# Decode attention with a gate and a Mish layer: all eight kv heads loaded alike, the dense layer's weights behind them, and wo split over three loads

## The chip, the cores and the metric

The kernel runs on one core of one Trainium2 chip. The metric is the device time of one execution in microseconds (us), the median of three runs. TensorE (PE in the profile) does the matmuls and the transposes, VectorE (DVE), ScalarE (ACT) and GpSimd (POOL) the rest, and SyncE (SP) issues every DMA. All inputs lie in HBM and are read once.

## The reference

Two tokens (B = 2, one position each) pass through an attention over the last W = 4096 positions of a cache and, beside it, through a dense layer with the Mish function; a sigmoid gate mixes the two.

```python
g = _sigmoid((x * gate_w).sum(-1, keepdims=True))
# attention: 32 query heads, 8 kv heads, head size 128, model size 512
q = (x @ wq).reshape(B, Sq, Hq, Dh)...
scores = jnp.einsum("bhqd,bhkd->bhqk", q, k) * (Dh ** -0.5)
o = jnp.einsum("bhqk,bhkd->bhqd", _softmax(scores), v)
a = o.reshape(B, Sq, Hq * Dh) @ wo
# dense layer: 512 -> 1792 -> 512
h = jnp.einsum("bsd,df->bsf", x, w1) + b1
b = jnp.einsum("bsf,fd->bsd", h * jnp.tanh(softplus(h)), w2)
return g * a + (1 - g) * b
```

Everything is 32-bit floating point, so the inputs that have to be moved are 91.24 MB.

## The kernel before

**Loads.** Everything large goes through one pool of three tiles of 64 KB on each of the 128 partitions (`stream`, the helper `load`). A `load` makes a tile and issues one DMA on SP for each of its parts. The eleven tiles come in this order: wq (two parts), kv0 to kv6 (one part of 64 KB rows each, keys in the first half, values in the second), then `w12`, which holds w1 and ten of the fourteen pieces of w2 (one part of 48 KB rows), then `kv7` in two parts of 32 KB rows (keys, values), then `wo` in three parts of 32, 24 and 8 KB rows (16, 12 and 4 query heads). The last four pieces of w2 are three more DMAs (4, 2 and 2 KB rows) into the room left behind in `w12`'s tile. With three tiles, the DMA of a tile waits until PE has read the tile three places ahead of it: w12's waits for kv4, kv7's for kv5, wo's for kv6. The table `CUTS` says how w2 is cut, `WO` how wo is cut (in groups of four query heads).

**A kv head.** `scores` makes the four score products `sc` (16 matmuls, in four column groups of PE that run side by side), the maximum `mx` on DVE and the exponentials `p` on ACT; `turned` transposes `p` on PE into `pp` and copies it to `pT` on ACT; `values` makes `o` (16 matmuls), and after each second head folds two heads into `od` on DVE. Each 32-bit matmul is two PE instructions in the profile, so 16 matmuls are x32 there.

**The dense layer.** `hidden` multiplies w1 into `hp` (16 matmuls), copies it on ACT (`hs`), transposes it (`ht`), and then runs a chain of small operations, mostly on POOL (`e`, `ho`, `nu`, `de`), that ends in the padded activations `actT` and `act2` (both in the tile `padded`).

**Joining the heads.** The chunks of each row of scores have their own maxima. `tops` transposes `mx` on PE into `mt`, finds the common maximum (`mj`, `top` on DVE), subtracts it on POOL (`ms`) and takes exponentials on ACT; `factors` transposes `ms` into `ft` and makes `kf` and `kl` on DVE; `shares` sums on PE into `lp` and makes `r` on DVE and POOL; `outputs` multiplies `od` by `kf` on PE into `ol` and writes the scaled heads `oT` (in `padded`) on DVE.

**The end.** `project` adds 32 query heads times wo and ten pieces of activation times w2 (`middle`) into `acc`, in four column groups, one for each index modulo 4. ACT copies `acc` to `asum`; `finish` adds the last four pieces of w2 and `asum` into `fin`, DVE copies it to `res`, and SP stores it once the last loads have landed.

**Order.** The engines run their instructions in program order; `pin` keeps the marked matmuls as written, the rest is placed by the framework's scheduler. In this kernel the work on w1 (`hidden`) comes ahead of kv7, and the ten `middle` pieces, `tops`, `factors` and `shares` are written by hand between the steps of kv7.

Of the kernel before, what the change touches and what calls it, by code (L numbers as in the profile page):

```python
# [8 lines left out]
F32 = mybir.dt.float32  # L9
AF = mybir.ActivationFunctionType  # L10
ALU = mybir.AluOpType
AX = mybir.AxisListType

P = 128
B = 2
D = 512
HQ = 32
HKV = 8
REP = HQ // HKV
# [6 lines left out]
NT = 4  # L26
Q = 32
RS = Q // B
BH = B * REP
F = 1792  # L30
DC = D // P
# [3 lines left out]
CHUNK = 8192  # L35
# [1 line left out]
SMALL = DC * B + DC + FC  # L37
SCALE = DH ** -0.5
CAP = 20.0
CUTS = (0, 10, 12, 13, 14)  # L40
WO = (0, 4, 7, 8)
ROWS = (24, 104)
WIDE = 2 * Q - B


@with_exitstack
def decode_kernel(ctx: ExitStack, tc: tile.TileContext, res, stored, small, wqh, wqt, kv_in, w12, k7, v7, wo, w2, out):
    nc = tc.nc

    stream = ctx.enter_context(tc.tile_pool(name="stream", bufs=3))  # L50
# [8 lines left out]
    def load(name, *parts):  # L59
        t = stream.tile([P, 2 * CHUNK], F32, tag="s", name=name)  # L60
        x = 0
        for cols, src in parts:
            loads.append(nc.sync.dma_start(t[:, x : x + cols], src))  # L63
            x += cols
        return t
# [12 lines left out]
    for j in range(2, NJ):  # L78
# [6 lines left out]
                            axis=AX.X, op=ALU.add)  # L85
# [54 lines left out]

    pin = tc.keep_in_program_order

    def scores(kv, t):
        sc = ps_s.tile([P, 512], F32, tag="sc", name=f"sc{kv}")
        for m in range(BN):
            for j in range(NJ):
                nc.tensor.matmul(sc[Q * j : Q * j + Q, :], qz[:, kv, m * Q : m * Q + Q],  # L147
                                 t[:, (m * NJ + j) * 512 : (m * NJ + j + 1) * 512],
                                 start=(m == 0), stop=(m == BN - 1))
        nc.vector.tensor_reduce(mx[:, kv : kv + 1], sc, axis=AX.X, op=ALU.max, negate=True)  # L150
        p = work.tile([P, 512], F32, tag="p", name=f"p{kv}")
        nc.scalar.activation(p, sc, AF.Exp, bias=mx[:, kv : kv + 1], accum_out=ls[:, kv : kv + 1])  # L152
        return p

    def turned(kv, p):
        pp = ps_1.tile([P, NT, P], F32, tag="pt", name=f"pp{kv}")
        pT = single.tile([P, NT, P], F32, tag="pT", name=f"pT{kv}")
        for c in range(NT):
            pin(nc.tensor.transpose(pp[:, c, :], p[:, c * P : (c + 1) * P], ident))  # L159
        nc.scalar.copy(pT, pp)  # L160
        return pT

    def softmax(kv, t):
        return turned(kv, scores(kv, t))

    pair = [None]

    def values(kv, pT, t, c0=0, c1=NT):
        if kv % 2 == 0:
            pair[0] = ps_1.tile([P, 2, BN * DH], F32, tag="o", name=f"o{kv}")  # L170
        o = pair[0][:, kv % 2, :]
        for c in range(c0, c1):
            for j in range(NJ):
                pin(nc.tensor.matmul(o[Q * j : Q * j + Q], pT[:, c, Q * j : Q * j + Q],  # L174
                                     t[:, (c * NJ + j) * 512 : (c * NJ + j + 1) * 512],
                                     start=(c == 0), stop=(c == NT - 1)))
        if kv % 2 and c1 == NT:
            wide = [P, 2 * BN, DH]
            om = single.tile(wide, F32, tag="om", name=f"om{kv}")
            ov = om.rearrange("p (k m) d -> p k m d", m=BN)  # L180
            nc.vector.tensor_tensor(  # L181
                ov, pair[0].rearrange("p k (m d) -> p k m d", m=BN),
                pick[:, None, :, None].to_broadcast([P, 2, BN, DH]), op=ALU.mult)
            nc.vector.tensor_reduce(od[:, kv - 1 : kv + 1], ov.rearrange("p k m d -> p k d m"),  # L184
                                    axis=AX.X, op=ALU.add)
# [34 lines left out]
        nc.gpsimd.tensor_tensor(r, r, g[:, None, :, None].to_broadcast([P, HKV, B, REP]), op=ALU.mult)  # L220
        return r

    def outputs(ol, kf, r, k0, k1):
        for kv in range(k0, k1):
            pin(nc.tensor.matmul(ol[:, kv].rearrange("p b h -> p (b h)"), od[:, kv, :], kf[:, kv, :],  # L225
                                 start=True, stop=True))
        nc.vector.tensor_tensor(
            oT.rearrange("p (k h) (b x) -> p k b h x", h=REP, x=RS)[:, k0:k1, :, :, 0],
            ol[:, k0:k1], r[:, k0:k1], op=ALU.mult)

    def hidden(t):
        w = t[:, : DC * F].rearrange("p (c f) -> p c f", c=DC)
        hp = ps_s.tile([P, FG * P], F32, tag="sc", name="hp")
        for c in range(DC):
            for j in range(NJ):
                n = min(FG, FC - j * FG) * P
                nc.tensor.matmul(hp[Q * j : Q * j + Q, :n], x32[:, c, :],  # L237
                                 w[:, c, j * FG * P : j * FG * P + n],
                                 start=(c == 0), stop=(c == DC - 1))
        hs = work.tile([P, FG * P], F32, tag="p", name="hs")  # L240
        nl = (FC - (NJ - 1) * FG) * P
        nc.scalar.copy(hs[:, :nl], hp[:, :nl])
        nc.scalar.copy(hs[: Q * (NJ - 1), nl:], hp[: Q * (NJ - 1), nl:])
        ht = ps_1.tile([P, FG, NJ, Q], F32, tag="pt", name="ht")

        def m(name):
            return const.tile([P, FC, B], F32, name=name)

        h, e, nu, de, ho = (m(x) for x in ("h", "e", "nu", "de", "ho"))
        for k in range(FG):  # L250
            nj = len(range(k, FC, FG))
            nc.tensor.transpose(ht[:, k, :nj, :].rearrange("p j r -> p (j r)"),
                                hs[: Q * nj, k * P : (k + 1) * P], ident[: Q * nj, : Q * nj])
        for j0, j1, nk in ((0, NJ - 1, FG), (NJ - 1, NJ, FC - (NJ - 1) * FG)):
            f0, f1 = j0 * FG, (j1 - 1) * FG + nk
            nc.vector.tensor_tensor(  # L256
                h[:, f0:f1, :].rearrange("p (j k) b -> p j k b", k=nk),
                ht[:, :nk, j0:j1, ::RS].rearrange("p k j b -> p j k b"),
                b1[:, f0:f1].rearrange("p (j k) -> p j k", k=nk)[:, :, :, None]
                .to_broadcast([P, j1 - j0, nk, B]), op=ALU.add)  # L260
        nc.gpsimd.tensor_scalar_min(e, h, CAP)  # L261
        nc.scalar.activation(e, e, AF.Exp)
        nc.gpsimd.tensor_tensor(ho, h, omg[:, None, :].to_broadcast([P, FC, B]), op=ALU.mult)
        nc.gpsimd.tensor_scalar_add(nu, e, 2.0)
        nc.gpsimd.tensor_tensor(nu, nu, e, op=ALU.mult)
        nc.gpsimd.tensor_scalar_add(de, nu, 2.0)
        nc.vector.reciprocal(de, de)
        nc.gpsimd.tensor_tensor(nu, nu, de, op=ALU.mult)
        nc.gpsimd.tensor_tensor(actT[:, :, ::RS], nu[:, : CUTS[1]], ho[:, : CUTS[1]], op=ALU.mult)
        nc.gpsimd.tensor_tensor(act2[:, :, Q - B : Q], nu[:, CUTS[1] :], ho[:, CUTS[1] :], op=ALU.mult)  # L270

    queries(0, wq_t[:, :CHUNK])
    queries(1, wq_t[:, CHUNK:])

    for kv in range(HKV - 1):
        t = load(f"kv{kv}", (2 * CHUNK, kv_in[kv]))
        pT = softmax(kv, t[:, :CHUNK])
        values(kv, pT, t[:, CHUNK:])
    w12_t = load("w12", (DC * F + CUTS[1] * D, w12))
    last = load("kv7", (CHUNK, k7), (CHUNK, v7))  # L280

    def flat(src, cuts, size):
        for f0, f1 in zip(cuts, cuts[1:]):
            yield (f1 - f0) * size, src[f0 * size * P : f1 * size * P].rearrange("(p x) -> p x", p=P)

    wo_t = load("wo", *flat(wo, WO, REP * D))
    x = DC * F + CUTS[1] * D
    for cols, src in flat(w2, [f - CUTS[1] for f in CUTS[1:]], D):
        loads.append(nc.sync.dma_start(w12_t[:, x : x + cols], src))
        x += cols  # L290
    hidden(w12_t)

    acc = ps_1.tile([P, D], F32, tag="acc", name="acc")
    fin = ps_1.tile([P, P], F32, tag="fin", name="fin")
# [17 lines left out]

    def middle(f0, f1):
        for f in range(f0, f1):
            x = DC * F + f * D
            pin(project(f % NJ, actT[:, f, :], w12_t[:, x : x + D], n_of[f % NJ]))

    p = scores(HKV - 1, last[:, :CHUNK])
    middle(0, CUTS[1] // 2)
    ms = tops()  # L320
    pT = turned(HKV - 1, p)
    middle(CUTS[1] // 2, CUTS[1])
    kf, kl = factors(ms)
    values(HKV - 1, pT, last[:, CHUNK:], 0, 1)
    r = shares(kl)
    values(HKV - 1, pT, last[:, CHUNK:], 1, NT)
    ol = ps_1.tile([P, HKV, B, REP], F32, tag="q", name="ol")
    outputs(ol, kf, r, 0, HKV - 2)
    outputs(ol, kf, r, HKV - 2, HKV)
    for x in range(HQ):  # L330
        project(x % REP, oT[:, x, :], wo_t[:, x * D : (x + 1) * D], n_of[x % REP])
    asum = work.tile([P, D], F32, tag="p", name="asum")
    nc.scalar.copy(asum, acc)

    def output(i):
        for f in range(CUTS[i], CUTS[i + 1]):
            x = DC * F + f * D
            finish(act2[:, f - CUTS[1], :], w12_t[:, x : x + D])

    output(1)  # L340
# [71 lines left out]
```

## Time and profile before

| | us |
|---|---|
| median of 3 runs (219.44 to 219.54) | 219.47 |
| the profiled execution's own time | 219.29 |
| its span, first to last instruction | 217.4 |
| last load lands, last `fin` matmuls wait for it | 215.0 |

The page gives, for each engine, its busy time and its share of the span; the chain that ended last, followed back from the last instruction; and groups of instructions by line with the idle time before them and what ended it. In a timeline row the first number is the start in us from the span's start, the second the duration, and a bracket at the end holds the idle time before it and its releaser. PEclk is the TensorE clock that was granted, 1.00 being full speed.

### The profile page before, as it was taken

What the parts mean: (1) busy time and instruction counts of PE and PEld (TensorE: products, weight loads), DVE (VectorE), ACT (ScalarE), POOL (GpSimd) and SP (SyncE); (2) the same over time, 40 slices, a digit from 0 to 9 for tenths busy, and PEclk for the clock granted to TensorE, in tenths of its full rate; (3) what the DMA queues carried; (4) which work ended last, traced back from release to release, by engine and by line L of the source; (5) the groups of instructions that cost most, each with busy time, mean ns of one, the idle gap of its engine ahead of it and who ended that gap; (6) DMA issues with size and microseconds to landing.
All of it is one profiled execution on the core that took longest, in us unless ns stands there. A gap on an engine that the chain in (4) does not pass through costs nothing.

```text
span 217.4 us, 1803 instructions
## 1 busy us (share of the span) xinstructions
PE 120.3 (55%) x804; PEld 34.5 (16%) x804; DVE 21.5 (10%) x33; ACT 15.6 (7%) x34; POOL 8.0 (4%) x30
## 2 busy tenths in 40 slices
PE   0000798377046609543873754287066972997766
PEld 0000322112011102101120210012011220233212
DVE  0000000010001230100105010010501000025100
ACT  2000001011001000200020020002001010030001
POOL 7000000000000000000000000000000003010000
PEclk9999999879959985995669699669758697699699
DMA  9797988898989899989998999899999899999993
GB/s 362 338 506 338 581 386 386 386 570 386 398 386 567 377 398 398 555 386 398 398 555 377 398 410 543 386 398 410 488 434 434 359 464 404 455 410 443 430 383 136
DMA packets 2838, 91.38 MB, mean 420 GB/s; under 512 B 448, under 2 KB 528, under 8 KB 912
## 3 DMA queue, kind: packets, MB, share of 16 engines
q1 hardware_dynamic: 2832, 91.28, 97.5%
q8 instruction: 6, 0.10, 0.2%
HBM read 91.24 MB, written 0.04 MB: 420 GB/s over the span
## 4 chain that ended last, share of the span: by engine, by line
DMA 76%; PE 18%; ACT 2%; DVE 1%; SPq 1%; issue 1%; ACTq 0%
DMA kv<-in_kv 60%; DMA wo<-in_wo 16%; PE sc L147 9%; PE o L174 6%; PE acc L299 2%; ACT p L152 1%; DVE mx L150 1%; PE pp L159 1%; ACT pT L160 1%; PE fin L309 1%; SPq L63 1%; SPq L69 0%; DVE res L350 0%; ACTq L160 0%; ACTq L152 0%
## 5 line engine op out<-in xcount | busy, mean ns | idle before, releaser
L147 PE MATMUL sc<-kv,qz 128*32 128x512 f32 x256 | 47.3, 907 | 49.0 <-DMA kv<-in_kv 44.2
L174 PE MATMUL o<-kv,pT 128*32 128x512 f32 x256 | 32.4, 647 | 5.1 <-ACT pT L160 5.1
L127 PE MATMUL qp<-wq,x 128*32 128x512 f32 x64 | 11.9, 790 | 23.0 <-POOL x L91 23.0
L147 PEld LDWEIGHTS sc<-kv,qz 128*32 128x32 f32 x256 | 10.5, 157 | 83.7 <-DMA kv<-in_kv 49.8
L150 DVE TENSOR_REDUCE mx<-sc 128x1 f32<-128x512 f32 x8 | 5.5, 692 | 102.3 <-PE sc L147 102.3
L152 ACT ACTIVATE p<-sc,mx 128x512 f32<-128x512 f32 x8 | 5.5, 687 | 126.4 <-DVE mx L150 126.4
L159 PE MATMUL pp<-ident,p 128*128 128x128 f32 x32 | 5.2, 285 | 11.6 <-ACT p L152 11.6
L174 PEld LDWEIGHTS o<-kv,pT 128*32 128x32 f32 x256 | 7.8, 118 | 23.2 <-issue 16.4
L299 PE MATMUL acc<-wo,padded 128*32 128x512 f32 x64 | 8.9, 705 | 2.3 <-DMA wo<-in_wo 2.3
L184 DVE TENSOR_REDUCE od<-om 128x256 f32<-128x1024 f32 x4 | 7.5, 1883 | 0.1
L127 PEld LDWEIGHTS qp<-wq,x 128*32 128x32 f32 x64 | 2.5, 136 | 29.0 <-POOL x L91 23.0
L181 DVE TENSOR_TENSOR om<-o,pick 128x1024 f32<-128x1024 f32 x4 | 4.9, 1224 | 21.6 <-PE o L174 21.6
L159 PEld LDWEIGHTS pp<-ident,p 128*128 128x128 f32 x32 | 3.4, 141 | 18.4 <-ACT p L152 18.4
L261 POOL TENSOR_SCALAR e<-h 128x28 f32<-128x28 f32 x1 | 0.3, 285 | 151.3 <-DVE h L256 151.3
L160 ACT COPY pT<-pp 128x512 f32<-128x512 f32 x8 | 4.7, 586 | 5.8 <-PE pp L159 5.8
L299 PE MATMUL acc<-w,padded 128*32 128x512 f32 x20 | 3.8, 597 | 0.0
L237 PE MATMUL hp<-w,x 128*32 128x512 f32 (+1 forms) x32 | 3.6, 540 | 0.0
L299 PEld LDWEIGHTS acc<-wo,padded 128*32 128x32 f32 x64 | 2.1, 126 | 8.3 <-issue 4.4
L225 PE MATMUL ol<-kf,od 128*128 128x8 f32 x16 | 2.1, 259 | 2.2 <-DVE od L184 2.2
L225 PEld LDWEIGHTS ol<-kf,od 128*128 128x128 f32 x16 | 1.9, 191 | 3.1 <-DVE od L184 2.3
L116 DVE RECIPROCAL g<-g 128x2 f32<-128x2 f32 x1 | 0.2, 166 | 22.5 <-POOL g L115 22.5
L133 PE MATMUL qt<-ident,qs 128*128 128x128 f32 x8 | 1.3, 286 | 1.4 <-ACT qs L130 1.4
(65 smaller groups left out, 29.8 us busy)
## 6 DMA issues: line engine op xcount, KB each, us to landing
wq<-in_wqt SPq DMA_DIRECT2D x1, 7168.0 KB, 21.4
w<-in_w SPq DMA_DIRECT2D x1, 6144.0 KB, 41.0
kv<-in_k SPq DMA_DIRECT2D x1, 4096.0 KB, 30.7
kv<-in_v SPq DMA_DIRECT2D x1, 4096.0 KB, 40.0
wo<-in_wo SPq DMA_DIRECT2D x1, 4096.0 KB, 28.7
wo<-in_wo SPq DMA_DIRECT2D x1, 3072.0 KB, 35.6
wq<-in_wqh SPq DMA_DIRECT2D x1, 1024.0 KB, 4.9
wo<-in_wo SPq DMA_DIRECT2D x1, 1024.0 KB, 37.5
```

Of the source, the lines that this page charges most:

```text
L127: nc.tensor.matmul(qp[Q * k : Q * k + Q, :], x32[:, c, :], w[:, c, k, :], start=(c == 0), stop=(c == DC - 1))
L147: nc.tensor.matmul(sc[Q * j : Q * j + Q, :], qz[:, kv, m * Q : m * Q + Q], t[:, (m * NJ + j) * 512 : (m * NJ + j + 1) * 512], start=(m == ...
L150: nc.vector.tensor_reduce(mx[:, kv : kv + 1], sc, axis=AX.X, op=ALU.max, negate=True)
L152: nc.scalar.activation(p, sc, AF.Exp, bias=mx[:, kv : kv + 1], accum_out=ls[:, kv : kv + 1])
L159: pin(nc.tensor.transpose(pp[:, c, :], p[:, c * P : (c + 1) * P], ident))
L160: nc.scalar.copy(pT, pp)
L174: pin(nc.tensor.matmul(o[Q * j : Q * j + Q], pT[:, c, Q * j : Q * j + Q], t[:, (c * NJ + j) * 512 : (c * NJ + j + 1) * 512], start=(c == 0 ...
L181: nc.vector.tensor_tensor(ov, pair[0].rearrange("p k (m d) -> p k m d", m=BN), pick[:, None, :, None].to_broadcast([P, 2, BN, DH]), op=ALU ...
L184: nc.vector.tensor_reduce(od[:, kv - 1 : kv + 1], ov.rearrange("p k m d -> p k d m"), axis=AX.X, op=ALU.add)
L225: pin(nc.tensor.matmul(ol[:, kv].rearrange("p b h -> p (b h)"), od[:, kv, :], kf[:, kv, :], start=True, stop=True))
L237: nc.tensor.matmul(hp[Q * j : Q * j + Q, :n], x32[:, c, :], w[:, c, j * FG * P : j * FG * P + n], start=(c == 0), stop=(c == DC - 1))
L299: return nc.tensor.matmul(acc[Q * j : Q * j + Q, :], lhsT, rhs, start=(n_col[j] == 1), stop=(n_col[j] == n))
```

## The change

kv7 becomes a tile like the others: one DMA of 64 KB rows right behind kv6. `w12` comes behind it, as one DMA of 54 KB rows: w1, then the first four query heads of wo (one kv head's group, `WO[0]` = 1), then nine pieces of w2. The other 28 query heads of wo are two DMAs of 40 and 16 KB rows (20 and 8 heads), and the last five pieces of w2 three DMAs of 6, 2 and 2 KB rows. `scores` and `turned` become one function again, and the hand-written order around kv7 goes: the program is now kv7, `hidden`, `tops`, `factors`, `shares`, `outputs` (all eight heads at once), then the matmuls into `acc` with `middle` behind the first four heads.

```diff
-CUTS = (0, 10, 12, 13, 14)
-WO = (0, 4, 7, 8)
+CUTS = (0, 9, 12, 13, 14)
+WO = (1, 6, 8)
...
+AHEAD = DC * F + WO[0] * REP * D
...
-    for kv in range(HKV - 1):
+    for kv in range(HKV):
         t = load(f"kv{kv}", (2 * CHUNK, kv_in[kv]))
         pT = softmax(kv, t[:, :CHUNK])
         values(kv, pT, t[:, CHUNK:])
-    w12_t = load("w12", (DC * F + CUTS[1] * D, w12))
-    last = load("kv7", (CHUNK, k7), (CHUNK, v7))
+    w12_t = load("w12", (AHEAD + CUTS[1] * D, w12))
...
-    wo_t = load("wo", *flat(wo, WO, REP * D))
-    x = DC * F + CUTS[1] * D
+    wo_t = load("wo", *flat(wo, [f - WO[0] for f in WO], REP * D))
+    x = AHEAD + CUTS[1] * D
...
     hidden(w12_t)
+    kf, kl = factors(tops())
+    outputs(kf, shares(kl))
...
-    p = scores(HKV - 1, last[:, :CHUNK])
-    middle(0, CUTS[1] // 2)
-    ms = tops()
-    pT = turned(HKV - 1, p)
-    middle(CUTS[1] // 2, CUTS[1])
-    kf, kl = factors(ms)
-    values(HKV - 1, pT, last[:, CHUNK:], 0, 1)
-    r = shares(kl)
-    values(HKV - 1, pT, last[:, CHUNK:], 1, NT)
-    ol = ps_1.tile([P, HKV, B, REP], F32, tag="q", name="ol")
-    outputs(ol, kf, r, 0, HKV - 2)
-    outputs(ol, kf, r, HKV - 2, HKV)
+    first = WO[0] * REP
     for x in range(HQ):
-        project(x % REP, oT[:, x, :], wo_t[:, x * D : (x + 1) * D], n_of[x % REP])
+        w = w12_t[:, DC * F + x * D :] if x < first else wo_t[:, (x - first) * D :]
+        if x == first:
+            middle(0, CUTS[1])
+        pin(project(x % REP, oT[:, x, :], w[:, :D], n_of[x % REP]))
```

PE before, from the end of `hidden` to the products with wo (`kv_499` is kv7's tile, `w_497` is w12's; a row counts matmuls, not the two instructions of each):

```order
L252 MATMUL ht<-ident,hs 128x96 x2
L147 MATMUL sc_553<-kv_499,qz 32x512 x16
L299 MATMUL acc<-w_497,padded 32x512 x5
L189 MATMUL mt<-ident,mx 8x128
L159 MATMUL pp_589<-ident,p_571 128x128 x4
L299 MATMUL acc<-w_497,padded 32x512 x5
L205 MATMUL ft<-ident,ms 128x8
L174 MATMUL o_480<-kv_499,pT_590 32x512 x4
L216 MATMUL lp<-kl,ones 128x64
L174 MATMUL o_480<-kv_499,pT_590 32x512 x12
L225 MATMUL ol<-kf,od 128x8 x8
L299 MATMUL acc<-wo,padded 32x512 x32
```

PE with the change, from the end of `hidden` to the end of the program (`w_545` is w12's tile):

```order
L247 MATMUL ht<-ident,hs 128x96 x2
L184 MATMUL mt<-ident,mx 8x128
L200 MATMUL ft<-ident,ms 128x8
L211 MATMUL lp<-kl,ones 128x64
L221 MATMUL ol<-kf,od 128x8 x8
L295 MATMUL acc<-w_545,padded 32x512 x13
L295 MATMUL acc<-wo,padded 32x512 x28
L305 MATMUL fin<-w_545,padded 32x128 x12
L305 MATMUL fin<-asum,padded 32x128 x4
L305 MATMUL fin<-w_545,padded 32x128 x8
```

All of kv7's matmuls have gone from between these rows to a place ahead of `hidden`, and the products with w2 that stood between them now stand, nine of them, behind `ol`. PE at that earlier place, with the change (`kv_497` is kv7's tile now):

```order
L148 MATMUL sc_499<-kv_497,qz 32x512 x16
L157 MATMUL pp_519<-ident,p_517 128x128 x4
L169 MATMUL o_480<-kv_497,pT_520 32x512 x16
L232 MATMUL hp<-w_545,x_93 32x512 x3
L232 MATMUL hp<-w_545,x_93 32x256
```

The product with w1 stands behind kv7, and before it stood ahead of it. POOL with the change, from the first operation of the Mish chain to the last of `shares`:

```order
L256 TENSOR_SCALAR e<-h 128x28
L258 TENSOR_TENSOR ho<-h,omg 128x28
L259 TENSOR_SCALAR nu<-e 128x28
L193 TENSOR_TENSOR ms<-ms,top 8x16x4
L260 TENSOR_TENSOR nu<-nu,e 128x28
L193 TENSOR_TENSOR ms<-ms,top 8x16x4
L261 TENSOR_SCALAR de<-nu 128x28
L263 TENSOR_TENSOR nu<-nu,de 128x28
L264 TENSOR_TENSOR padded<-nu,ho 128x18
L265 TENSOR_TENSOR padded<-nu,ho 128x5x2
L215 TENSOR_TENSOR r<-r,g 128x64
```

The two subtractions into `ms` now stand among the operations of the Mish chain; before, they came behind all of them. On SP the two rows of kv7 become one row ahead of w12's, and the three rows of wo become two.

More of the change, by code (lines that the diff above doesn't have):

```diff
@@ L39, with decode_kernel @@
 CAP = 20.0
-CUTS = (0, 10, 12, 13, 14)
-WO = (0, 4, 7, 8)
+CUTS = (0, 9, 12, 13, 14)
+WO = (1, 6, 8)
 ROWS = (24, 104)
 WIDE = 2 * Q - B
+AHEAD = DC * F + WO[0] * REP * D
 @with_exitstack
-def decode_kernel(ctx: ExitStack, tc: tile.TileContext, res, stored, small, wqh, wqt, kv_in, w12, k7, v7, wo, w2, out):
+def decode_kernel(ctx: ExitStack, tc: tile.TileContext, res, stored, small, wqh, wqt, kv_in, w12, wo, w2, out):
     nc = tc.nc
@@ L141, in decode_kernel, with softmax @@
     pin = tc.keep_in_program_order
-    def scores(kv, t):
+    def softmax(kv, t):
         sc = ps_s.tile([P, 512], F32, tag="sc", name=f"sc{kv}")
@@ L152, in scores @@
         nc.scalar.activation(p, sc, AF.Exp, bias=mx[:, kv : kv + 1], accum_out=ls[:, kv : kv + 1])
-        return p
-    def turned(kv, p):
         pp = ps_1.tile([P, NT, P], F32, tag="pt", name=f"pp{kv}")
@@ L161, in turned, with values @@
         return pT
-    def softmax(kv, t):
-        return turned(kv, scores(kv, t))
     pair = [None]
-    def values(kv, pT, t, c0=0, c1=NT):
+    def values(kv, pT, t):
         if kv % 2 == 0:
@@ L171, in values @@
         o = pair[0][:, kv % 2, :]
-        for c in range(c0, c1):
+        for c in range(NT):
             for j in range(NJ):
@@ L176, in values @@
                                      start=(c == 0), stop=(c == NT - 1)))
-        if kv % 2 and c1 == NT:
+        if kv % 2:
             wide = [P, 2 * BN, DH]
@@ L221, in shares, with outputs @@
         return r
-    def outputs(ol, kf, r, k0, k1):
-        for kv in range(k0, k1):
+    def outputs(kf, r):
+        ol = ps_1.tile([P, HKV, B, REP], F32, tag="q", name="ol")
+        for kv in range(HKV):
             pin(nc.tensor.matmul(ol[:, kv].rearrange("p b h -> p (b h)"), od[:, kv, :], kf[:, kv, :],
@@ L227, in outputs @@
         nc.vector.tensor_tensor(
-            oT.rearrange("p (k h) (b x) -> p k b h x", h=REP, x=RS)[:, k0:k1, :, :, 0],
-            ol[:, k0:k1], r[:, k0:k1], op=ALU.mult)
+            oT.rearrange("p (k h) (b x) -> p k b h x", h=REP, x=RS)[:, :, :, :, 0], ol, r, op=ALU.mult)
     def hidden(t):
@@ L273, in decode_kernel @@
     queries(1, wq_t[:, CHUNK:])
-    for kv in range(HKV - 1):
+    for kv in range(HKV):
         t = load(f"kv{kv}", (2 * CHUNK, kv_in[kv]))
@@ L314, in middle @@
         for f in range(f0, f1):
-            x = DC * F + f * D
+            x = AHEAD + f * D
             pin(project(f % NJ, actT[:, f, :], w12_t[:, x : x + D], n_of[f % NJ]))
-    p = scores(HKV - 1, last[:, :CHUNK])
-    middle(0, CUTS[1] // 2)
-    ms = tops()
-    pT = turned(HKV - 1, p)
-    middle(CUTS[1] // 2, CUTS[1])
-    kf, kl = factors(ms)
-    values(HKV - 1, pT, last[:, CHUNK:], 0, 1)
-    r = shares(kl)
-    values(HKV - 1, pT, last[:, CHUNK:], 1, NT)
-    ol = ps_1.tile([P, HKV, B, REP], F32, tag="q", name="ol")
-    outputs(ol, kf, r, 0, HKV - 2)
-    outputs(ol, kf, r, HKV - 2, HKV)
+    first = WO[0] * REP
     for x in range(HQ):
-        project(x % REP, oT[:, x, :], wo_t[:, x * D : (x + 1) * D], n_of[x % REP])
+        w = w12_t[:, DC * F + x * D :] if x < first else wo_t[:, (x - first) * D :]
+        if x == first:
+            middle(0, CUTS[1])
+        pin(project(x % REP, oT[:, x, :], w[:, :D], n_of[x % REP]))
     asum = work.tile([P, D], F32, tag="p", name="asum")
@@ L336, in output @@
         for f in range(CUTS[i], CUTS[i + 1]):
-            x = DC * F + f * D
+            x = AHEAD + f * D
             finish(act2[:, f - CUTS[1], :], w12_t[:, x : x + D])
@@ L381 @@
     wo = a("A_wo").reshape(HQ, DH, D)
+    wo_0 = wo[: WO[0] * REP].transpose(1, 0, 2).reshape(P, WO[0] * REP * D)
     wo = np.concatenate([wo[f * REP : t * REP].transpose(1, 0, 2).ravel()
@@ L389 @@
         "wqt": c(wq[:, HEAD:]),
-        "kv": c(np.concatenate([kt[:-1], vt[:-1]], axis=2)),
-        "w12": c(np.concatenate([w1, w2_0], axis=1)),
-        "k7": c(kt[-1]),
-        "v7": c(vt[-1]),
+        "kv": c(np.concatenate([kt, vt], axis=2)),
+        "w12": c(np.concatenate([w1, wo_0, w2_0], axis=1)),
         "wo": c(wo),
```

## Prediction

> **What bounds the kernel now.** I read the page first: its span, the DMA queues and the chain that ended last.
>
> ```profile
> span 217.4 us, 1803 instructions
> q1 hardware_dynamic: 2832, 91.28, 97.5%
> DMA 76%; PE 18%; ACT 2%; DVE 1%; SPq 1%; issue 1%; ACTq 0%
> ```
>
> The loads keep the 16 DMA engines busy for 97.5% of the span. The kernel is one stream of 91.28 MB, and PE works on what has landed. So two questions decide: when each tile lands, and how much work is left behind the last tiles. For the landings, here are rows of SP's timeline, of the list of DMA issues (the last number is the time from issue to landing) and of the chain.
>
> ```profile
> 132.79 0.33 SPq L63 DMA_DIRECT2D w<-in_w  x1
> 152.70 0.33 SPq L63 DMA_DIRECT2D kv<-in_k  x1
> 153.08 0.54 SPq L63 DMA_DIRECT2D kv<-in_v  x1
> 174.13 1.28 SPq L63 DMA_DIRECT2D wo<-in_wo  x3
> ```
> ```profile
> w<-in_w SPq DMA_DIRECT2D x1, 6144.0 KB, 41.0
> kv<-in_k SPq DMA_DIRECT2D x1, 4096.0 KB, 30.7
> kv<-in_v SPq DMA_DIRECT2D x1, 4096.0 KB, 40.0
> wo<-in_wo SPq DMA_DIRECT2D x1, 4096.0 KB, 28.7
> out<-res SPq DMA_DIRECT2D x1, 40.0 KB, 1.5
> ```
> ```profile
> 116.11 43.20 DMA kv<-in_kv
> 174.50 35.56 DMA wo<-in_wo
> 210.11 3.64 PE acc L299 x32
> 213.78 0.65 PE fin L309 x16
> 214.46 1.05 PE fin L309 x24
> 215.53 0.29 DVE res L350
> ```
>
> kv6 lands at 116.11 + 43.20 = 159.3, w12 at 132.79 + 41.0 = 173.8, kv7's keys at 183.4 and values at 193.1, the first part of wo at 174.13 + 28.7 = 202.8, the second at 174.50 + 35.56 = 210.1. Every step is rows times about 0.302 us for each KB of the row: 48 KB in 14.5, 32 KB in 9.6 to 9.7, 24 KB in 7.2. All were issued 28 us or more before they landed, so the stream has no gap.
>
> The end shows how well PE keeps up. `acc` ends at 210.11 + 3.64 = 213.75, and this row shows that the last weights of `fin` still waited for the last load, 215.0:
>
> ```profile
> 215.04 0.16 PEld L309 LDWEIGHTS fin<-w,padded 128*32 128x32 f32 x8 [0.21 <-DMA w<-in_w]
> ```
>
> So before the change PE is just ahead of the stream, with 0.2 us to spare. The end is 215.0 plus the last `fin`, `res` and the store.
>
> **The change, in the stream.** The same bytes move, in two DMAs fewer. What a DMA costs beside its bytes is bounded by the rows above: keys and values together took 193.1 - 173.8 = 19.3 us for 64 KB, a rate at which w12's 48 KB would take 14.5, as they did. Two fewer save between 0 and 0.2 us; I take 0.1. The landings after the change follow from 0.302 us a KB: kv7 at 159.3 + 19.3 = 178.6, **w12 at 178.6 + 16.3 = 194.9**, wo's first part (40 KB) at 207.0, its second (16 KB) at 211.8, the last load at 214.9. SP issues kv7, w12 and wo when it issued w12, kv7 and wo (PE's release of kv4, kv5, kv6 does not move), so the queue stays full.
>
> The Trainium skill, "DMA: Bandwidth & Descriptors", section on the anatomy of one DMA, fits a fixed cost of about 2.0 us for each DMA, on the path that software feeds. By it, one DMA fewer ahead of w12 would move all that follows by 2 us; keys and values, at 9.6 to 9.7 us each beside 19.3 for a whole kv tile, show no such cost in this queue.
>
> **The change, on PE.** w12 used to land at 173.8, ahead of kv7, so `hidden` and ten `middle` pieces were done while kv7 came in. Now it lands at 194.9, last but for wo, and everything below waits for it in a row, with 20.0 us to the last landing. Rows of PE's timeline (start, duration), of DVE's and of POOL's:
>
> ```profile
> 159.36 6.51 PE L147 MATMUL sc<-kv,qz 128*32 128x512 f32 x32 [6.72 <-DMA kv<-in_kv]
> 168.89 5.17 PE L174 MATMUL o<-kv,pT 128*32 128x512 f32 x32 [0.73 <-ACT pT L160]
> 173.88 3.60 PE L237 MATMUL hp<-w,x 128*32 128x512 f32 x32
> 177.99 0.65 PE L252 MATMUL ht<-ident,hs 128*128 128x128 f32 x4 [0.51 <-ACT hs L242]
> 189.71 1.88 PE L299 MATMUL acc<-w,padded 128*32 128x512 f32 x10
> 191.52 0.27 PE L189 MATMUL mt<-ident,mx 128*8 128x128 f32 x1
> 194.00 0.22 PE L205 MATMUL ft<-ident,ms 8*128 8x8 f32 x1
> 195.15 0.43 PE L216 MATMUL lp<-kl,ones 128*128 128x64 f32 x2
> 198.22 1.50 PE L225 MATMUL ol<-kf,od 128*128 128x8 f32 x12
> 201.90 0.61 PE L225 MATMUL ol<-kf,od 128*128 128x8 f32 x4 [2.17 <-DVE od L184]
> ```
> ```profile
> 194.51 0.22 DVE L211 TENSOR_TENSOR kl<-kf,ls 128x64 f32<-128x64 f32 x1
> 199.84 0.24 DVE L227 TENSOR_TENSOR padded<-ol,r 128x48 f32<-128x48 f32 x1 [0.25 <-PE ol L225]
> ```
> ```profile
> 192.76 0.59 POOL L198 TENSOR_TENSOR ms<-ms,top 8x64 f32<-8x64 f32 x2 [10.98 <-DVE top L196]
> ```
>
> kv7 itself is not on the path: kv6 took from 159.3 to 168.89 + 5.17 = 174.1, 14.8 us, so kv7 is through by 178.6 + 14.8 = 193.4 at the latest. From 194.9 on, step by step:
>
> 1. `hp`: 3.6 us at full clock. The same 32 instructions of `sc` took 6.5 where the clock was 0.50, so the other end is 6.8. I take **5.5**, for the reason under the clock below.
> 2. `hs` and `ht`: from `hp`'s end, 177.48, to `ht`'s, 178.64: **1.15**.
> 3. `mt` to `ft`: `ft` began 2.5 us after `mt` began. Now `ms` shares POOL with the Mish chain: its two subtractions (0.59 back to back) stand behind three operations and have a fourth between them, which adds about 0.5; the `mt` itself is ready when `ht` ends. I take 2.7 from `ht`'s end.
> 4. `ft` to `kl`'s end: 0.73; the reciprocal of the Mish chain may stand ahead of `kf` on DVE, 0.1 more. So `lp` begins 3.55 after `ht`.
> 5. `ol`: its first instruction comes 0.3 behind `lp`'s first, twelve took 1.50, sixteen take 1.95. These were hidden behind `om` and wo's landing before; now the product with wo waits for all of them. Then the scaling on DVE, 0.24 and a gap. `oT` stands **6.1** after `ht` (5.7 to 6.6 if the interleaving on POOL costs less or more). The `r` branch, 0.43 of `lp` and two short operations, is done a microsecond earlier.
> 6. `acc`: four matmuls on different column groups run side by side, so 32 instructions are 8 slots of 0.43 (3.60 us), and five pieces take 4 slots (1.88 us), the fifth being alone. 4 heads, 9 pieces and 28 heads are 2 + 6 + 14 = 22 slots: 9.6 us at full clock. By then wo's first part has landed (207.0); its second (211.8) is there before PE needs it. I take **10.8**. Queued behind are all of `fin`, `asum`, `res` and the store.
> 7. From `acc`'s end: `asum` and the `fin` matmuls, 214.46 - 213.75 = 0.71, then 1.05 less the 0.21 of waiting, then from 215.51 to 217.4: **3.4**.
>
> **The clock.** TensorE's clock is granted in steps of 3.41 us in this trace. I laid windows on these steps; the columns are the stretch, its length, PE's busy time and instructions, the granted clock, the DMA share and GB/s.
>
> ```profile
> 182.25:185.66 3.41, 2.17 (x12) 0.50 1.07 461
> 185.66:189.08 3.42, 3.42 (x20) 0.50 1.00 426
> 199.32:202.73 3.41, 1.02 (x8) 1.00 0.99 425
> 202.73:206.14 3.41, 3.31 (x16) 0.50 1.00 432
> 206.14:209.56 3.42, 1.95 (x20) 1.00 0.93 393
> 209.56:212.97 3.41, 2.86 (x28) 1.00 0.99 406
> ```
>
> A stretch with 1.02 us of work at full clock is followed by half, one with 1.95 by full; at half clock 2.17 is not enough to get full back, 3.31 is. With the change PE rests 1.5 us or more ahead of `hp`, and has little to do for the 7.2 us of steps 2 to 5 (`ht`, `mt`, `ft`, `lp`, `ol`: 3.5 us together). So I expect `hp` at half clock for part of its way (5.5) and `acc` to begin with some 2.4 us at half, which costs half of that, 1.2. Where the steps fall against the work is not known, and this is the larger part of the range.
>
> The Trainium skill, "TensorE: Matmul & The Clock Gate", Part 1, has the clock go to half after at least one idle window of about 3.4 us. Here PE rested only from 199.7 to 201.9 (rows of `ol`), 2.2 us, and half was granted at 202.73 all the same, so by this trace a thinly used window is enough. By the page's rule `acc` would start at full clock, since no step from 2 to 5 leaves PE idle for 3.4 us; that is a rival below.
>
> **Sum.** 194.9 + 5.5 + 1.15 + 6.1 + 10.8 + 3.4 = 221.9 for the span, against 217.4. The profiled execution took 219.29, 1.9 more than its span, and the median is 0.2 above it: 221.9 + 2.1 = **224.0**. With all low ends (3.6, 5.7, 9.6) it is 220.5; with all high ends (6.8, 6.6, and 13.0 for `acc` with 6.8 us at half) 228.0.
>
> **The rivals.**
>
> - *PE keeps full clock* through `hp` and `acc` (3.6 and 9.6): 194.9 + 3.6 + 1.15 + 6.1 + 9.6 + 3.4 = 218.8, time 220.9. For it: a short rest may leave a step busy enough, as 206.14 shows; against it: 199.32. This is also where the page's rule leads when PE's rest ahead of `hp` stays short. Chance 0.10.
> - *Half clock for long*, `hp` all at half and `acc` for two steps (6.8 and 13.0): 225.4, time 227.5. For it: a step that is half full stays at half (182.25). Chance 0.10.
> - *The stream still sets the end*, that is, PE's row fits between w12's landing and the last load: 217.3, time 219.4, not slower. Its place is step 6, and it decides from this point: `acc` must end by about 213.8, 18.9 us behind w12, where the low ends of steps 1 to 6 add up to 20.1. It needs steps 3 to 5 to take 4.5 us instead of 6.1, at full clock throughout. Before the change they took 8.3 us from `mt` (191.52) to the first scaling (199.84), with kv7's matmuls in between, so little speaks for it. Chance 0.06, of which 0.02 for a gain over 0.2% from the two DMAs saved and a luckier stream.
> - *Fewer DMAs speed the stream* by the page's 2 us ahead of w12: 222.0. Against it: 9.6 to 9.7 beside 19.3. Chance 0.02.
> - *The forecast*, 222.3 to 225.7 with the clock somewhere between: 0.72.
>
> **How the numbers follow.** The range goes from 220.8, the full clock throughout, to 226.2; it leaves out the longest half clock (0.10) and the stream (0.06). A measurement of this kernel can tell about 0.2% from no change. Faster by more than that 0.02, within it 0.04, slower 0.94.
>
> **What would show it.** In the profile after: `hp` starts at about 194.9 and waits for `w<-in_w`; `acc<-w` starts between 205.5 and 209.5 and waits for DVE's `padded`; `acc<-wo` waits for no load or hardly; the last load lands at about 214.9 with no matmul waiting for it; PEclk is 0.50 in a step near 196 to 200 and in one near 206 to 210. The prediction is wrong if `acc` ends before 214, or if w12 lands well away from 194.9.

## The result and the profile after

The changed kernel takes 225.72 us (median of 6 executions, 224.65 to 227.76), the kernel before 219.45 (219.21 to 219.54): a ratio of 1.0294, 95% interval 1.0247 to 1.0341. It is slower by about 6.3 us. The profiled execution of the changed kernel took 224.65 us, the fastest of the six, with a span of 222.8. In the ratios and medians below, single executions more than 1.5% above the fastest of their kernel are left out (225.46, 225.9, 244.07 and 575.63 us).

The page after, with the same three rows as before:

```profile
span 222.8 us, 1812 instructions
q1 hardware_dynamic: 2544, 91.28, 95.2%
DMA 70%; PE 24%; ACT 2%; DVE 1%; POOL 1%; issue 1%; SPq 0%; ACTq 0%; DVEq 0%
```

The same 91.28 MB keep the DMA engines busy for the same time, but of a longer span, and PE's share of the chain has gone up from 18 to 24%. The end of the chain that ended last, in order of time (start, duration, what):

```profile
151.80 43.18 DMA w<-in_w
195.03 3.69 PE hp L232 x11
...
199.16 0.67 PE ht L247 x4
...
202.25 0.24 PE ft L200
...
203.15 0.42 PE lp L211 x2
203.59 0.57 DVE r L214
204.20 3.38 PE ol L221 x16
207.68 0.28 DVE padded L223
208.00 11.32 PE acc L295 x80
219.34 0.59 ACT asum L321
219.98 0.91 PE fin L305 x24
220.91 0.29 DVE res L338
```

From w12's landing at 151.80 + 43.18 = 194.98 on there is no DMA left in the chain: the steps follow each other without a load between them. Before, the chain went from kv6 through wo's second part, landing at 210.07. The loads, from SP's timeline and the list of DMA issues (the last number is issue to landing):

```profile
171.79 0.81 SPq L64 DMA_DIRECT2D wo<-in_wo  x2
172.65 1.41 SPq L283 DMA_DIRECT2D w<-in_w  x3
```
```profile
wo<-in_wo SPq DMA_DIRECT2D x1, 5120.0 KB, 35.3
w<-in_w SPq DMA_DIRECT2D x2, 256.0 KB, 41.3
```

wo's first part landed at 171.79 + 35.3 = 207.1, and the last pieces of w2 some 41.3 us after issues between 173 and 174, about 215, as before. The stream is as long as it was; `acc` is still at work 4 us later.

The clock in windows of its 3.41 us steps (columns as in the prediction):

```profile
194.23:197.64 3.41, 2.61 (x28) 1.00 1.25 541
197.64:201.05 3.41, 1.78 (x14) 1.00 0.94 408
201.05:204.47 3.42, 0.90 (x6) 1.00 0.89 383
204.47:207.88 3.41, 3.10 (x16) 0.50 0.91 392
207.88:211.30 3.42, 3.30 (x16) 0.50 0.96 408
211.30:214.71 3.41, 3.41 (x36) 1.00 0.67 263
```

`hp` ran at full clock in this execution. The thin step 201.05 to 204.47 (0.90 us of work) was followed by half clock, and so was the next one, although `ol` filled 3.10 us of it.

### The profile page after: what moved, and what is told of

It reads as the page before. It is cut to its first block, busy times and chain, and to the rows that moved or that the text cites. A ratio compares the mean times of both kernels' runs of the same rounds, so it can differ in the third digit from the quotient of the medians.

```text
span 222.8 us, 1812 instructions
## 1 busy us (share of the span) xinstructions
PE 122.0 (55%) x810; PEld 36.5 (16%) x810; DVE 21.6 (10%) x32; ACT 15.6 (7%) x34; POOL 7.9 (4%) x30
## 3 DMA queue, kind: packets, MB, share of 16 engines
q1 hardware_dynamic: 2544, 91.28, 95.2%
## 4 chain that ended last, share of the span: by engine, by line
DMA 70%; PE 24%; ACT 2%; DVE 1%; POOL 1%; issue 1%; SPq 0%; ACTq 0%; DVEq 0%
DMA kv<-in_kv 41%; DMA w<-in_w 19%; DMA sm<-in_small 9%; PE acc L295 5%; PE qp L128 5%; PE sc L148 5%; PE o L169 3%; PE hp L232 2%; PE ol L221 2%; PE zp L112 1%; ACT p L153 1%; DVE mx L151 1%; PE pp L157 1%; ACT pT L158 1%; PE fin L305 0%
## 5 line engine op out<-in xcount | busy, mean ns | idle before, releaser
L169 PE MATMUL o<-kv,pT 128*32 128x512 f32 x256 | 34.7, 692 | 5.8 <-ACT pT L158 5.8
L128 PE MATMUL qp<-wq,x 128*32 128x512 f32 x64 | 11.0, 733 | 23.1 <-POOL x L92 23.1
L169 PEld LDWEIGHTS o<-kv,pT 128*32 128x32 f32 x256 | 8.4, 126 | 26.8 <-issue 19.1
L295 PE MATMUL acc<-wo,padded 128*32 128x512 f32 x56 | 7.0, 594 | 0.0
L295 PE MATMUL acc<-w,padded 128*32 128x512 f32 x26 | 5.2, 864 | 0.4 <-DVE padded L223 0.4
L221 PE MATMUL ol<-kf,od 128*128 128x8 f32 x16 | 3.4, 349 | 0.7 <-DVE r L214 0.7
L221 PEld LDWEIGHTS ol<-kf,od 128*128 128x128 f32 x16 | 3.3, 312 | 0.8 <-DVE r L214 0.8
## 6 DMA issues: line engine op xcount, KB each, us to landing
wo<-in_wo SPq DMA_DIRECT2D x1, 5120.0 KB, 35.3
w<-in_w SPq DMA_DIRECT2D x2, 256.0 KB, 41.3
```

The source lines that it names most:

```text
L128: nc.tensor.matmul(qp[Q * k : Q * k + Q, :], x32[:, c, :], w[:, c, k, :], start=(c == 0), stop=(c == DC - 1))
L295: return nc.tensor.matmul(acc[Q * j : Q * j + Q, :], lhsT, rhs, start=(n_col[j] == 1), stop=(n_col[j] == n))
```

## Experiments

Theory A: the row of PE work that stands behind w12's landing sets the end, and the loads themselves cost nothing. Theory B: the new stream (order, row sizes, two DMAs fewer) sets it. Theory C: only PE's clock is to blame.

**The same loads, another order of work.** The loads, cuts and tiles of the change stay; kv7's work gets the hand-written order that it had before, and only `hidden` and `outputs` are left behind w12 (`p` is what `scores` returns for kv7).

```diff
+    ms = tops()
+    pT = turned(kv, p)
+    kf, kl = factors(ms)
+    values(kv, pT, t[:, CHUNK:], 0, 1)
+    r = shares(kl)
+    values(kv, pT, t[:, CHUNK:], 1, NT)
...
     hidden(w12_t)
-    kf, kl = factors(tops())
-    outputs(kf, shares(kl))
+    outputs(kf, r)
```

> The loads and cuts of the change, and the hand-written order of before inside kv7: tops behind its scores, factors behind pp, shares behind the first quarter of its values; then hidden, outputs and the products. Theory A: hp starts at 195.0, ol right behind ht, acc at 202 to 203; PE is done with what has landed before wo's second part, the last fin waits for the last load again, and the time is 219.2 to 220.0, the same as before within 0.3%. Theory B: about 225.7, since the loads are those of the change. Theory C: 223 or more.

Measured: 219.34 us, ratio to the kernel before 1.0011 (0.9991 to 1.0031). Three of 12 executions took more than 219.8 (220.16, 220.5, 221.8). Its page and PE's timeline:

```profile
span 217.4 us, 1812 instructions
q1 hardware_dynamic: 2544, 91.28, 97.6%
```
```profile
184.87 0.27 PE L187 MATMUL mt<-ident,mx 128*8 128x128 f32 x1 [0.82 <-DVE mx L151]
...
187.43 0.22 PE L203 MATMUL ft<-ident,ms 8*128 8x8 f32 x1 [1.09 <-ACT ms L198]
...
195.10 5.33 PE L235 MATMUL hp<-w,x 128*32 128x512 f32 x32 [3.38 <-DMA w<-in_w]
...
201.42 1.88 PE L224 MATMUL ol<-kf,od 128*128 128x8 f32 x16
203.72 3.67 PE L304 MATMUL acc<-w,padded 128*32 128x512 f32 x26 [0.43 <-DVE padded L226]
207.03 4.66 PE L304 MATMUL acc<-wo,padded 128*32 128x512 f32 x40
211.87 1.92 PE L304 MATMUL acc<-wo,padded 128*32 128x512 f32 x16 [0.18 <-DMA wo<-in_wo]
```

w12 lands when it did in the changed kernel (`hp` starts at 195.10), and `hp` is even slower here, 5.33 us. But `mt` stands at 184.87, not at 199.65, `ol` follows right behind `ht`, `acc` begins 4.3 us earlier than in the changed kernel, and its last part waits for wo again. In the median all of the loss is gone with the loads unchanged: B falls, and A holds. The wait for the stream that shows is that of `acc` for wo's second part (0.18), not one of the last `fin`. C falls as the whole account. Half clock cost the changed kernel 1.4 us in `ol` and 1.7 in `acc`, of the 5.4 us between the profiled executions of before and after; here it cost `hp` 1.7 us, and the time still came back.

**A coarser way to do the same.** `tops`, `factors` and `shares` are called just ahead of `hidden`, after all of kv7.

```diff
+    kf, kl = factors(tops())
+    r = shares(kl)
     hidden(w12_t)
-    kf, kl = factors(tops())
-    outputs(kf, shares(kl))
+    outputs(kf, r)
```

> The changed kernel with tops, factors and shares called ahead of hidden, outputs behind it; loads and everything else as changed. Theory A: hp starts about 2 us late (lp stands ahead of it on PE), but oT follows ht after some 2.3 us instead of 8; acc starts near 204 and the time is 219.5 to 222. Theory B: no change, since the loads are the same. Theory C: no change beyond the clock's scatter, 224.5 to 227.8.

Measured: 220.32 us in the median of three executions, ratio 1.0041 (1.0027 to 1.0056). Most of the loss comes back with two calls moved; about 1 us is left. A fourth execution took 225.46, as long as the changed kernel, and it is the only one with a trace:

```profile
193.27 0.27 PE L184 MATMUL mt<-ident,mx 128*8 128x128 f32 x1
197.85 0.23 PE L200 MATMUL ft<-ident,ms 8*128 8x8 f32 x1 [4.31 <-ACT ms L195]
...
199.33 6.41 PE L232 MATMUL hp<-w,x 128*32 128x512 f32 x32
```

The join now stands ahead of `hp` on PE, and it waits for DVE, which folds two heads (`om`, `od`) before it finds `top`. So `hp` begins at 199.33, 4.3 us later than in the changed kernel and not the 2 us expected, and it runs mostly at half clock. How long `hp` was held up in the three shorter executions is not shown.

**One part undone.** w12 is loaded ahead of kv7 again and `hidden` comes ahead of kv7's work; the rest is the changed kernel.

```diff
+    w12_t = load("w12", (AHEAD + CUTS[1] * D, w12))
+    last = load("kv7", (2 * CHUNK, kv_in[HKV - 1]))
...
     hidden(w12_t)
+    values(HKV - 1, softmax(HKV - 1, last[:, :CHUNK]), last[:, CHUNK:])
     kf, kl = factors(tops())
```

> One part of the change undone: w12 is loaded ahead of kv7 again, and hidden stands ahead of kv7's work; the cuts, kv7 as one load and the straight order of the rest stay. Theory A (what counts is the row of PE work behind the last large tile): kv7 lands at 194.9 and now has its whole row behind it, scores to values 12 to 15 us, the join 10 us, acc 10 to 11 us, the tail 3.4, so the time goes up to 233 to 237. Rival theory (w12 landing late is in itself the loss): the time falls back towards 219.5.

Measured: 235.94 us, ratio 1.0773 (1.0735 to 1.0812). PE's timeline:

```profile
194.99 5.63 PE L148 MATMUL sc<-kv,qz 128*32 128x512 f32 x32 [14.53 <-DMA kv<-in_kv]
...
207.27 0.27 PE L184 MATMUL mt<-ident,mx 128*8 128x128 f32 x1
211.85 0.22 PE L200 MATMUL ft<-ident,ms 8*128 8x8 f32 x1 [4.30 <-ACT ms L195]
...
214.04 3.58 PE L221 MATMUL ol<-kf,od 128*128 128x8 f32 x16 [0.65 <-DVE r L214]
218.05 5.60 PE L297 MATMUL acc<-w,padded 128*32 128x512 f32 x25 [0.43 <-DVE padded L223]
```

With kv7 last, its whole row stands behind 194.9, and `acc` begins at 218.05. So loading w12 behind kv7 is not what costs: given the straight order of the code and kv7 as one load, it is the cheaper of the two orders of loads, by some 10 us. The 4.6 us from `mt` to `ft` also show that the join waits here: DVE has the folding of two heads (`om`, `od`) ahead of it.

**One part alone.** The kernel before, with kv7 as one load of 64 KB rows behind w12.

```diff
-    last = load("kv7", (CHUNK, k7), (CHUNK, v7))
+    last = load("kv7", (2 * CHUNK, kv_in[HKV - 1]))
```

> The kernel before with one part of the change: kv7 is one load of 64 KB rows, still behind w12; everything else as before. Theory A: kv7's keys are there at 193.1 instead of 183.4, all of PE's work from sc on moves by 9.6 us, acc ends at 219.6 to 221.3 and the time is 225 to 227. Rival (one load fewer speeds the stream): 219.3.

Measured: ratio 1.0168 (1.0148 to 1.0188), about 3.7 us slower, with a median of 222.84. The direction is A's, the size a miss. PE's timeline:

```profile
193.26 5.16 PE L147 MATMUL sc<-kv,qz 128*32 128x512 f32 x32 [14.53 <-DMA kv<-in_kv]
...
206.77 1.50 PE L225 MATMUL ol<-kf,od 128*128 128x8 f32 x12
208.68 1.90 PE L299 MATMUL acc<-wo,padded 128*32 128x512 f32 x10 [0.41 <-DVE padded L227]
...
211.06 5.78 PE L299 MATMUL acc<-wo,padded 128*32 128x512 f32 x51
```

The kernel before, for the same products:

```profile
183.49 6.39 PE L147 MATMUL sc<-kv,qz 128*32 128x512 f32 x32 [4.85 <-DMA kv<-in_k]
...
202.83 5.26 PE L299 MATMUL acc<-wo,padded 128*32 128x512 f32 x32 [0.32 <-DMA wo<-in_wo]
```

`sc` starts 9.8 us later than before (193.26, 183.49), `ol` 8.6 later (206.77, 198.22), and `acc` ends only some 3.5 later: wo has landed by then, so the products with it run on without the waits that they had before. The clock helped too: before, the first 32 instructions of `acc` with wo took 5.26 us, partly at half clock, and the next 32 took 3.64; here the clock was full from 196.38 on. A delay of PE is paid only from the point where it has used up the waits behind it.

**The two sizes that were off.** The next three runs look at `ol` and the clock. First, `ol` in another PSUM slot:

```diff
-        ol = ps_1.tile([P, HKV, B, REP], F32, tag="q", name="ol")
+        ol = ps_1.tile([P, HKV, B, REP], F32, tag="o", name="ol")
```

> One edit to the changed kernel: ol takes the PSUM slot of o instead of that of lp, so that it need not wait until the reciprocal has read lp. Theory A (PE's row of work behind w12's landing sets the end, and the wait for r is a part of it): ol starts 0.6 to 0.8 us earlier after kl, and the time falls by about 0.7 us to 225.0, within the scatter of the clock. Theory B (the stream of loads with its new rows sets the end): no change, and the last fin waits for a load. Theory C (only PE's clock is to blame): no change beyond the clock's scatter.

Measured: 226.1 us (224.14 to 227.19), ratio 1.0320 (1.0301 to 1.0340): no gain that its time could show. PE's timeline of its profiled execution (span 222.2):

```profile
203.45 0.41 PE L211 MATMUL lp<-kl,ones 128*128 128x64 f32 x2 [0.66 <-DVE kl L206]
203.69 2.56 PE L221 MATMUL ol<-kf,od 128*128 128x8 f32 x16
```

The wait is gone: `ol` starts 0.24 behind `lp`, where it started 1.05 behind it. In the changed kernel `ol` waited for DVE's `r` because it takes the PSUM slot of `lp`, which `r` reads. The gain of 0.8 us is smaller than the scatter between executions, so the trace shows it and the time doesn't.

Second and third, PE was given products of constants between `mt`, `ft`, `lp` and `ol`, in the changed kernel and in the one with the other slot (the three calls stand at the end of `tops`, behind `ft` in `factors` and behind `lp` in `shares`):

```diff
+    def warm(n, cols):
+        t = ps_s.tile([P, 512], F32, tag="sc", name="warm")
+        q = qz.rearrange("p k x -> p (k x)")
+        for _ in range(n):
+            for j in range(NJ):
+                pin(nc.tensor.matmul(t[Q * j : Q * j + Q, :cols], x32[:, j, :], q[:, :cols], start=True, stop=True))
...
+        warm(2, 512)
...
+        warm(1, 256)
...
+        warm(1, 256)
```

> The changed kernel with idle PE filled: products of constants into a spare score tile stand between mt and ft, ft and lp, lp and ol (48 more instructions, some 2.5 us of PE at full clock). Theory A with the clock as its second part: PEclk stays at 1.00 from hp to the end, ol takes 2.0 us instead of 3.4 and acc 9.6 to 10 instead of 11.3, so the span falls to about 219.8 and the time to 221.5 to 223, still slower than before. Theory C (only the clock): the time comes back to 219.5. Theory B: no change.

> The two edits to the changed kernel together: ol in the slot of o, and the products of constants between mt, ft, lp and ol. What it tells is how ol and acc run where the step of the clock before them was filled. If the granted clock were ruled by PE's busy time as the profile counts it, acc would start at full clock behind 2 us of ol; in the run with the products alone acc began at half clock behind a step filled with ol. Theory A': the narrow products of ol do not count for the clock, so acc starts at half clock again wherever a step of 3.41 us held ol and little else. The time is 221.5 to 224.5, slower than before in any case.

Measured: ratios 1.0192 (1.0148 to 1.0236) and 1.0227 (1.0208 to 1.0246), medians 223.76 and 224.43: the first above the range expected, the second inside it, near its upper end. The products of constants are 32 instructions and 3.2 us in the second's trace, where the first expectation has 48 and 2.5. In both traces `acc` began at half clock, where the first expectation had full clock to the end. The first's trace was granted 0.85 of the clock at most, so PE's timeline and the windows are those of the second:

```profile
205.96 1.95 PE L231 MATMUL ol<-kf,od 128*128 128x8 f32 x16
208.34 4.89 PE L305 MATMUL acc<-w,padded 128*32 128x512 f32 x25 [0.42 <-DVE padded L233]
```
```profile
202.30:205.71 3.41, 2.83 (x35) 1.00 0.86 370
205.71:209.12 3.41, 2.98 (x32) 1.00 0.98 418
209.12:212.53 3.41, 3.41 (x20) 0.50 0.93 387
```

With the step ahead of it filled (2.83 us), `ol` took 1.95 us, where it took 3.37 at half clock: its sixteen instructions come 0.11 us apart at full clock and 0.21 at half. But the step 205.71 to 209.12 counts 2.98 us of busy PE, 1.95 of them `ol`, and half clock followed all the same, so `acc` lost its 1.7 us as before. What fills a step by the profile's busy time need not keep the clock; `ol`, with 8 columns to a product, hardly did (the last section counts this over more steps). By the ratios, against those without the filling (1.0294 and 1.0320), it gained some 2 us, not the whole loss.

**A version with room to spare.** The loads of the change, the order of before inside kv7, and six of the eight `ol` products ahead of `hidden`. The lines shown are changes to the run that joined the heads inside kv7:

```diff
+    ol = ps_1.tile([P, HKV, B, REP], F32, tag="q", name="ol")
+    outputs(ol, kf, r, 0, HKV - 2)
     hidden(w12_t)
-    outputs(kf, r)
+    outputs(ol, kf, r, HKV - 2, HKV)
```

> The loads of the change with the order of before inside kv7, as in the run that joined the heads inside kv7, and six of the eight ol products ahead of hidden, where PE is idle. Theory A: four instead of sixteen instructions of ol are left behind w12, acc starts 1.5 us earlier or more, the last fin waits for the last load in nearly every execution: 219.2 to 219.4, with hardly an execution over 219.8. If the stream did gain from the change's two DMAs fewer it would be under 219.2.

Measured: 219.45 us, ratio 1.0013 (0.9996 to 1.0030); 2 of 11 executions took more than 219.8 (220.85 and 220.98). PE's timeline:

```profile
201.45 0.54 PE L223 MATMUL ol<-kf,od 128*128 128x8 f32 x4
201.92 1.07 PE L306 MATMUL acc<-w,padded 128*32 128x512 f32 x8
204.66 2.76 PE L306 MATMUL acc<-w,padded 128*32 128x512 f32 x18 [1.68 <-POOL padded L267]
```

`acc` begins at 201.92, 6 us earlier than in the changed kernel, and then waits 1.68 us for the Mish chain on POOL. This version is as fast as the kernel before and not faster: both stand at the stream. That hardly an execution would be over 219.8 was a miss: 2 of 11 were, beside 3 of 12 with all of `ol` behind w12. Why some executions of it, and of the run that joined the heads inside kv7, take a microsecond or two more was not traced; the clock's steps against the work are the likely cause, argued and not shown.

## Why the prediction was right

The time, 225.72, lies in the range (220.8 to 226.2), above the 224.0 forecast and near the upper end; three of the six executions lie beyond it (226.23, 226.24, 227.76). The mechanism is the one forecast: PE's row behind w12's landing sets the end. Point by point, in the profiled execution:

- *The stream.* w12 was forecast at 194.9 and landed at 194.98, wo's first part at 207.0 and landed at 207.1, and no matmul of the end waited for a load. Two DMAs fewer saved nothing that can be seen. The rival of 2 us for each DMA saved falls with it. That is the fixed cost that the Trainium skill, "DMA: Bandwidth & Descriptors", section on the anatomy of one DMA, gives for the other path; in this queue the landings show none of it.
- *Step 1, `hp`:* forecast 5.5, measured 3.63 (195.03 to 198.66). PE kept full clock, so the half clock named as a sign for 196 to 200 did not show. In the run that joined the heads inside kv7 the same instructions took 5.33, so half clock occurs too. PE's rest ahead of `hp` does not tell the two apart: it was 2.0 us here, and 1.75 in the run with `ol` split, where `hp` took 5.33 as well.
- *Step 2:* 1.15, as forecast. *Steps 3 and 4:* `lp` 3.55 behind `ht`'s end, measured 203.15 - 199.81 = 3.34.
- *Step 5, `ol`, is the term that was mis-sized:* `oT` was forecast 6.1 behind `ht` and stood at 8.1 (207.95). Two things were missed. `ol` was put 0.3 behind `lp`, but it waits for `r`, since both sit in one PSUM slot: 1.05 instead. And its 1.95 us was priced from rows at full clock; at half it took 3.37. The Trainium skill, "TensorE: Matmul & The Clock Gate", Part 2, section on LDWEIGHTS, prices a load of weights by its columns at a fixed 1.2 GHz; for 128 columns that is an estimate of 0.107 us. That is the spacing of `ol` at full clock here, 0.11; at half it was 0.21, so by this trace the granted clock governs it as well.
- *Step 6, `acc`:* forecast 10.8 with 2.4 us at half clock, measured 208.00 to 219.32 with 3.3 us at half. *Step 7:* forecast 3.4, measured 3.4.
- *The sum* was 221.9 for the span and came out at 222.8: 1.9 less in step 1, 2.0 more in step 5, 0.5 more in step 6, and 0.3 in the landing, the gaps and the tail. Two misses of equal size and opposite sign made the forecast look better than its parts; that is luck.
- *The median* lies 1.1 us above the profiled execution; the forecast added 0.2. Executions of the changed kernel spread over 3.1 us, where those of before spread over 0.3. As I read it, the stream hid PE's clock before, and nothing hides it now; the slower executions were not traced.
- *The rivals.* Full clock throughout did not happen: the step 201.05 to 204.47 held 0.90 us of work and was followed by half. By the rule of the Trainium skill, "TensorE: Matmul & The Clock Gate", Part 1, a whole idle window is needed for that; the longest rest there was 2.33 us (ahead of `ft`), so this trace disagrees. That the stream still sets the end was wrong for this kernel, and became true as soon as steps 3 and 4 were taken from behind w12; `ol` could stay there.

## What to carry to other kernels

In this kernel, bound by one stream, the order of the loads showed no price of its own; what counted is how much dependent work stands behind the last large tile, and the tile could move back for nothing only once work that doesn't need it stood ahead of it in the program. When loads are reordered, ask for each engine which instructions now stand behind the later landing without needing it: here the whole join of the heads, some 8 us, needed only kv7 and what came before it. And price work at the end of a row at half clock as well as at full, the small products included.

## What the runs showed of the hardware that was not expected

- Sixteen 32-bit matmul instructions with 128 weight columns and 8 moving columns took 1.95 us at full granted clock and 3.37 at half.
- In these traces such products did not keep or raise the clock: a 3.41 us step with 3.10 us of them at half clock was followed by half, and one with 1.95 us of them and 1.0 us of other work at full clock was followed by half, where other steps with 1.78 us of work (with `hp` and transposes) were followed by full.
- Counted over the 272 steps at full clock, from 40 us on, in the nine traces that reached full clock there: the 180 followed by full held at least 1.41 us of PE work other than `ol`, the 92 followed by half at most 1.63. The step with 1.95 us of `ol` is one of the 92, and so is one of the run with the join ahead of `hidden`, with 2.90 us of work, 1.64 of it `ol`.
